# A block's MLP as half products beside the scores of the next block's attention, with four maxima a group there

## The chip, the cores and the metric

The program runs on one core of one Trainium2 chip. The metric is the device time of one execution in microseconds (us), as the median of several runs; lower is better. The engines named below are PE (TensorE, matrix products), DVE (VectorE), ACT (ScalarE), POOL (GpSimd) and SP (the queue that issues most transfers). PEld is the loading of weights into PE.

## The reference

The reference is one transformer layer with a norm ahead of each half. `x` has 2048 rows of 512 numbers. All matrices are float32.

```
h  = x + attention(layernorm(x), wqkv) @ wo     # 32 heads of 16, full softmax over 2048 keys
h2 = h + silu(layernorm(h) @ w1) @ w2           # w1: 512 x 1792, w2: 1792 x 512
```

The kernel keeps float32 accuracy by splitting each float32 matrix of the MLP into a high and a low float16 part, and it takes three products for one (high by high, low by high, high by low). The softmax subtracts a row's maximum, and the kernel finds that maximum by computing the scores once more with queries on the partitions.

## The kernel before

**Blocks, items and groups.** The 2048 rows of queries are four blocks of 512. An *item* is one block of queries with four heads: 8 items a block, 32 in all. An item has 16 *groups*, one for each 128 keys, so there are 512 groups, and the main loop at the end of the kernel function runs over them in order.

**What one group does.** `scores` computes four products of 128 keys by 512 queries, one for each head. Each contracts over 64 rows, and it lies on the lower half of PE's rows (partitions 0 to 63) or on the upper half (64 to 127) by its head. Two products on different halves can run at the same time. Each score is followed by an exponential on ACT that reads the product from PSUM and writes a float32 tile named `pt` of 128 by 512. `maximum` computes a product of another, later item on 48 rows of the other half (the names in the profile are ps<-ks,qs for it and ps<-qs,ks for the score), and DVE reduces it to maxima. `values` multiplies the four `pt` tiles of the group two back (LAG = 2) by the values, in four column strips of PE that run together, and adds the result up in one bank of PSUM for the 16 groups of an item. Up to three maxima stand in a group, by the rate that `maxima` works out from when each item's maxima are due.

**PSUM.** There are eight banks. Scores take turns in a ring of four (`st`), maxima in a ring of three (`sm`), and one bank holds the sum of `values`. A product waits until the reading of what stood in its bank is done.

**The pt tiles.** `pt_tile` hands out 16 slots (PTS), 8 in one pool and 8 in another, in the order in which the tiles are asked for.

**The output and the MLP of a block.** When a block's eight items are done, the first item of the next block has eight groups (c of 8 to 15) with output work between their scores: product with `wo`, residual, statistics, norm, transposition by DMA into `hts`. Then `mlp` runs alone, with no exponentials: 14 first products of 12 matmuls, a SiLU and a split for each, then 4 row tiles of 42 matmuls. Into this stretch pairs of maxima are woven, 386 in all for the three stretches. ACT changes its function table for SiLU and back. The stretch stands before groups 144, 272 and 400 (`marks`). The fourth block's MLP runs at the end of the program, in `finish_last`.

**Order.** Every engine's instructions are kept in the order in which the code records them, and the tile framework adds the semaphores. An engine runs its queue in order, so an instruction that waits holds those behind it. SP issues transfers in order as well.

Of the kernel before, what the change touches and what calls it, by code (L numbers as in the profile page):

```python
# [20 lines left out]
P = 128  # L21
S = 2048
D = 512
# [25 lines left out]
PTS = 16  # L49
# [16 lines left out]
JOINT = 2  # L66
AHEAD = 4
# [4 lines left out]
BESIDE = (138, 138, 110)  # L72
OUTPUT = 8

# [7 lines left out]

BURSTS_1 = ({f: 6 for f in range(FC) if f not in (6, 13)},) * 2 + ({f: 6 for f in range(FC) if f % 3 != 1},)
BURSTS_2 = 12, 12, 10
SPAN_2 = 12 * (FC - 2) - 3

MORE = 2, 2, 0
# [3 lines left out]
def attention_mlp_kernel(ctx: ExitStack, tc: tile.TileContext, x, wqkv, wo, w1, w2, out):  # L91
# [5 lines left out]
    def mm(*a, **k):  # L97
        tc.keep_in_program_order(nc.tensor.matmul(*a, **k))  # L98
# [12 lines left out]
    def act(fn, *a, **k):  # L111
        pin(getattr(nc.scalar, fn)(*a, **k))  # L112
# [80 lines left out]
    factors = const.tile([P, 14], F32, name="factors")  # L193
    sigma, inverse = factors[:, :4], factors[:, 4:8]
    w1_s, w2_s, wo_s, o_s = (sigma[:, n:n + 1] for n in range(4))
    h_f, g_s, out_f, wo_f, o_minus, o_twice = (factors[:, n:n + 1] for n in range(8, 14))
# [141 lines left out]
    def place_far(piece):  # L338

        i, _ = piece  # L340
        mt = small.tile([P, 32], F16, name="mt")
        dve("transpose", mt, split.pop(piece))
        issue = dma_beside if at["beside"] else dma
# [27 lines left out]
    at = {"item": 0, "done": 0, "half": 0, "step": 0, "due": 0, "attention": False, "group": None, "ready": 0, "next": 0, "blocks": True, "beside": False}  # L371
# [21 lines left out]
    def found_maxima(piece):  # L393
        g = at["group"]
        marked = g is not None and g + 1 in marks
        if g is None or marked or piece[1] is None and start_of(piece) - g > FAR:
            soon(WAIT + 1 if g is None or marked else CALM, place_far, piece)
            finish_max(piece, marked)
            return
# [62 lines left out]
    def scores(g, k, kind="st"):  # L462
# [7 lines left out]
        pts[g, k] = pt_tile("pt")  # L470
        act("activation", pts[g, k], ps, AF.Exp, scale=qk_f)


    with ExitStack() as pa:
# [57 lines left out]
        def set_factors():  # L532
# [4 lines left out]
            for to, a, f in ((h_f, inverse[:, :1], 1 / LN), (g_s, w1_s, 1 / 32.0), (o_minus, o_s, -1.0),  # L537
# [269 lines left out]
        def begin_scores(n):  # L807

            for _ in range(n):
                g, k = first_scores.pop(0)  # L810
                scores(g, k, "sm")
# [37 lines left out]
    gp = ctx.enter_context(tc.tile_pool(name="gp", bufs=2))  # L849

# [23 lines left out]
    def finish_item(i):  # L874
# [6 lines left out]
        elif i in FIRSTS:  # L881
# [98 lines left out]
    first_weights = {9: ("w1", 0), 12: ("w1", 1), 14: ("w1", 2), 15: ("w1", 3)}  # L980
    order = [(kind, f) for kind in ("w1", "w2") for f in range(FC)]

# [49 lines left out]
    def load_rows(b, t):  # L1032
        n = 4 * b + t
        hx[t] = cpool.tile([P, D], F32, name="hx", bufs=4)
# [41 lines left out]
    def add_seconds(b, t, ps, m=0, parts=1):  # L1076
# [4 lines left out]
        (dma_beside if m or at["beside"] else dma)(out[n * P:(n + 1) * P, cols], h[:, cols])  # L1081

    def pair_seconds(b, acc, tiles, f, gates):

        w2 = [ws.pop(("w2", k)) for k in (f, f + 1)]
        for t in tiles:
            rows = slice(t * P, (t + 1) * P)
            for k, ((gh, gl), (w2h, w2l)) in enumerate(zip(gates[f:f + 2], w2)):
                for x, w in ((gh, w2h), (gl, w2h), (gh, w2l)):
                    mm(acc[t], x[:, rows], w, start=f + k == 0 and w is w2h and x is gh, stop=f + k == FC - 1 and w is w2l)  # L1090
                    yield
            if f + 2 == FC:
                add_seconds(b, t, acc[t])

    def last_seconds(b, acc, gates, inserts={}, tiles=range(4)):

        w2 = [ws.pop(("w2", f)) for f in range(FC - len(gates), FC)]
        k = 0
        if b == NB - 1:
            h = rows_of(b, 3)  # L1100
            dve("scalar_tensor_tensor", h, acc[3], out_f, h, op0=ALU.mult, op1=ALU.add)
        for t in tiles:
            rows = slice(t * P, (t + 1) * P)
            parts = 1 + (4 * b + t == KC - 1)
            for m in range(parts):
# [3 lines left out]
                for (gh, gl), (w2h, w2l) in zip(gates, w2):  # L1109
                    for x, w in ((gh, w2h), (gl, w2h), (gh, w2l)):  # L1110
                        mm(ps, x[:, rows], w[:, cols], start=first and parts == 2, stop=w is w2[-1][1])
                        first = False
                        k += 1
                        if k in inserts:
                            inserts[k]()
                add_seconds(b, t, ps, m, parts)

    def mlp(b):

        ahead = [(g, m ^ (g % 2)) for g in marks[b:b + 1] + [marks[b] + 1] for m in range(4)]  # L1120
        weights = iter(order[5:] + order[FC:])

        def next_weights():
            for kind, f in weights:
                load_weights(kind, f)
                return

        def some_scores(n):
            for _ in range(n):
                scores(*ahead.pop(0), "sm")  # L1130

        gates = []
        lay_out(st=range(4), sm=attention_banks)
        for f in range(FC):
            tick()
            next_weights()
            w1h, w1l = (w.rearrange("p (c n) -> p c n", n=P) for w in ws.pop(("w1", f)))
            ps = space[:, f % 2, :]
            n = BURSTS_1[b].get(f, 0)
            if f == 0:  # L1140
                burst(n, 4, 6, 2)
                n = 0
            weave(product(ps, lambda c: w1h[:, c, :], lambda c: w1l[:, c, :],
                          lambda c: hth[:, c, :], lambda c: htl[:, c, :], DC),
                  {6: lambda: burst(n, 4, 6, 2)} if n else {})
            gates.append(gate(ps, "pool"))

        act("activation", small.tile([P, 1], F32, name="sw"), ident[:, :1], AF.Exp)
        acc = [space[:, n, :] for n in range(4)]
        positions = {SPAN_2 * (n + 1) // BURSTS_2[b]: n for n in range(BURSTS_2[b])}  # L1150

        def insert(k):
            half = 12 * FC // 2
            pairs = (4, 6)
            if not (half - 12 < k < half + 12 or k == SPAN_2):
                pairs = (2 if k < half else 0), 4, 6
            burst(2 * len(pairs), *pairs)

        k = 0
        for part in range(2):  # L1160
            for f in range(0, FC - 4 * part, 2):
                at["beside"] = part == 0 or f < 4
                tick()
                next_weights()
                next_weights()
                for _ in pair_seconds(b, acc, (2 * part, 2 * part + 1), f, gates):
                    k += 1
                    if k in positions:
                        insert(k)
        for _ in range(2):  # L1170
            tick()
            next_weights()
            next_weights()

        def scores_in(*ring):
            lay_out(sm=ring)
            some_scores(4)

        last_seconds(b, acc, gates[-4:], {6: lambda: scores_in(0, 1, 4, 5), 18: lambda: scores_in(6, 7, 4, 5)}, (2, 3))
        lay_out(sm=attention_banks[:3])  # L1180

    found = {}

    def output(b, n):

        if n < 4:
            ps = bank()
            weave(project_rows(n, ps), {6: lambda: singles(3)} if n < MORE[b] else {})
# [15 lines left out]
    def finish_block(b, pending):  # L1204

        act("activation", small.tile([P, 1], F32, name="sw"), ident[:, :1], AF.Silu)
        load_weights("w1", 4)
        for g in pending:
# [241 lines left out]
```

## Time and profile before

| what | us |
|---|---|
| median of 3 runs | 1593.77 (1593.76 to 1594.98) |
| span of the profiled execution | 1591.2 |
| PE busy | 1579.5 (99%) |
| DVE busy | 1386.9 (87%) |
| ACT busy | 1205.0 (76%) |
| POOL busy | 484.8 (30%) |

The page has one profiled execution. Its own time is its span from the first to the last instruction, 1591.2 us; the timed runs have 2.6 us more around that. In its rows a matmul counts as busy for as long as it is in the array, and matmuls overlap, so a busy PE isn't a PE at its peak. A row of the timeline has the start, the length, the engine, the line, the operation, what is written and read, and how many equal instructions it merges. The granted TensorE clock is 1.0 over the whole span.

### The profile page before, as it was taken

To read this page: it belongs to the slowest core of one execution; us is meant where nothing else is said; L and a number is where in the kernel's file an instruction comes from. 1 tells how busy PE (TensorE), PEld (TensorE's weight loads), DVE (VectorE), ACT (ScalarE), POOL (GpSimd) and SP (SyncE) were. 2 spreads that over 40 slices of the span, in tenths; PEclk is the share of its full clock that TensorE was granted. 3 is DMA by queue.
4 is the path that set the end of the run, shared out by engine and by line. 5 is a ranking of instruction groups with operands and counts; after the bars stand their busy time and mean duration, and the time that the engine had idled before them with its cause. 6 is when DMAs were issued, how large, how long until landed. Compare 5 with 4: busy or idle time off the path is not lost. (4 is left out here: it accounts for less than half of the span.)

```text
span 1591.2 us, 28420 instructions
## 1 busy us (share of the span) xinstructions
PE 1579.5 (99%) x10476; PEld 471.7 (30%) x10476; DVE 1386.9 (87%) x2045; ACT 1205.0 (76%) x2384; POOL 484.8 (30%) x764
## 2 busy tenths in 40 slices
PE   9999999999999999999999999999999999999999
PEld 6434222222223322222224322222224322222254
DVE  7999999999998889999988889999986889998432
ACT  6545799999964179999973179999974189999732
POOL 5643544544446101211146101211146101211200
PEclk9999999999999999999999999999999999999999
DMA  6667533443443511121243521112143511100232
GB/s 216 174 177 221 136 86 91 113 119 86 116 100 102 157 47 35 38 51 44 50 102 101 152 53 34 39 41 53 48 104 108 159 40 37 34 12 22 74 87 73
DMA packets 124099, 140.29 MB, mean 88 GB/s; under 512 B 41808, under 2 KB 78736, under 8 KB 123960
## 3 DMA queue, kind: packets, MB, share of 16 engines
q1 hardware_dynamic: 117744, 128.34, 30.5%
q10 hardware_dynamic: 6216, 10.15, 2.3%
q8 instruction: 82, 1.34, 0.4%
q14 instruction: 57, 0.47, 0.1%
HBM read 104.68 MB, written 24.85 MB: 81 GB/s over the span
## 5 line engine op out<-in xcount | busy, mean ns | idle before, releaser
L112 ACT ACTIVATE pt<-ps 128x512 f32<-128x512 f32 x2048 | 1009.3, 611 | 154.4 <-PE ps L98 154.0
L301 DVE TENSOR_REDUCE mx<-ps 128x1 f32<-128x512 f32 x1470 | 925.1, 684 | 48.2 <-PE ps L98 20.3
L98 PE MATMUL ps<-pt,va 128*17 128x512 f32 x4096 | 537.5, 598 | 1.1
L98 PE MATMUL ps<-qs,ks 64*128 64x512 f16 x2048 | 530.9, 379 | 1.5 <-DMA qs<-mn 0.4
L98 PE MATMUL ps<-ks,qs 48*128 48x512 f16 x2048 | 495.4, 380 | 2.6 <-ACT pvs L112 1.1
L299 DVE TENSOR_REDUCE mx<-ps 128x2 f32<-128x1024 f32 x289 | 334.9, 1219 | 43.8 <-PE ps L98 42.5
L98 PEld LDWEIGHTS <-ks 64*128 64x128 f16 x2048 | 149.3, 95 | 549.2 <-issue 432.5
L105 POOL TENSOR_TENSOR ri<-rc,minus 128x16 f32<-128x16 f32 x31 | 90.7, 2926 | 242.5 <-DMA rc<-dn 192.3
L98 PE MATMUL ps<-w,gh 128*128 128x512 f16 (+1 forms) x678 | 154.4, 378 | 0.0
L98 PE MATMUL ps<-hts,w 128*128 128x512 f16 (+1 forms) x708 | 153.3, 369 | 0.0
L98 PEld LDWEIGHTS <-qs 48*128 48x128 f16 x2048 | 126.1, 94 | 77.5 <-issue 61.3
L98 PEld LDWEIGHTS ps<-pt,va 128*17 128x17 f32 x4096 | 69.0, 95 | 225.7 <-issue 205.4
L112 ACT ACTIVATE g<-ps,factors 128x512 f32<-128x512 f32 x56 | 38.4, 686 | 125.0 <-PE ps L98 95.7
L105 POOL TENSOR_TENSOR mx<-mx 128x32 f32<-128x32 f32 x52 | 12.6, 241 | 386.4 <-DVE mx L301 379.8
L98 PEld LDWEIGHTS <-w 128*128 128x128 f16 x708 | 66.5, 98 | 78.6 <-issue 10.2
L98 PEld LDWEIGHTS <-gh 128*128 128x128 f16 x678 | 63.1, 98 | 82.9 <-issue 13.7
L112 ACT ACTIVATE ks<-ps 128x512 f32<-128x512 f32 x30 | 17.9, 598 | 50.5 <-PE ps L98 45.1
L115 DVE SCALAR_TENSOR_TENSOR gh<-g,factors,gh 128x512 f16<-128x512 f32 x14 | 10.5, 751 | 52.1 <-ACT gh L112 52.1
L105 POOL TENSOR_TENSOR sl<-ks,sh 128x512 f16<-128x512 f32 x30 | 34.7, 1157 | 51.5 <-ACT sh L112 38.1
L105 POOL TENSOR_TENSOR gh<-g,gh 128x512 f16<-128x512 f32 x42 | 48.6, 1156 | 3.5
L105 POOL TENSOR_TENSOR ot<-ot,den 128x512 f32<-128x512 f32 (+1 forms) x16 | 20.4, 1273 | 84.4 <-DMA den<-dr 75.8
L98 PE MATMUL ps<-xth,wqk_h 128*128 128x512 f16 x120 | 45.8, 381 | 0.0
(155 smaller groups left out, 919.7 us busy)
## 6 DMA issues: line engine op xcount, KB each, us to landing
w<-w2d SPq DMA_DIRECT2D x98, 256.0 KB
ks<-kd SPq DMA_DIRECT2D x120, 192.0 KB
w<-w1d SPq DMA_DIRECT2D x56, 256.0 KB
ks<-in_B_w_dram ACTq DMA_DIRECT2D x28, 256.0 KB
w<-in_B_w_dram SPq DMA_DIRECT2D x28, 256.0 KB
qs<-qd SPq DMA_DIRECT2D x128, 48.0 KB
kd<-sh SPq DMA_DIRECT2D x16, 256.0 KB
qd<-sh SPq DMA_DIRECT2D x16, 256.0 KB
```

The source lines that it names most:

```text
L98: tc.keep_in_program_order(nc.tensor.matmul(*a, **k))
L105: tc.keep_in_program_order(getattr(nc.gpsimd, op)(*a, **k))
L112: pin(getattr(nc.scalar, fn)(*a, **k))
L115: pin(getattr(nc.vector, fn)(*a, **k))
L299: pin(nc.vector.tensor_reduce(of, space[:, n:n + 2, :], axis=AX.X, op=ALU.max))
L301: pin(nc.vector.tensor_reduce(of[:, j:j + 1], space[:, n, :], axis=AX.X, op=ALU.max))
```

## The change

The three MLP stretches are gone. A block's MLP runs instead inside 112 groups of the next block, from the same three marks on (groups 144 to 255, 272 to 383, 400 to 511). They are called *MLP groups* here, and the other 176 *plain groups*.

Each product of the MLP over 128 rows is made of two *half products* over 64 rows each, which add into one bank (bank 3). In an even group six half products run on the lower row half, and in the odd group after it the same six run on the upper half. The scores of the two groups are sorted for this: the even group takes the four scores on the upper half, two of its own and two of the next group, and the odd group takes the four on the lower half. A group's matmuls are recorded as pairs, one from each half. With four maxima that makes seven such pairs, where before there were four.

Since two halves must not write a bank at one time, the first half product of a group waits for the exponential of the last score of the group ahead (`after`, the entry "fence"). Where a chain ends, ACT copies the bank out and the next chain's first half product waits for that copy.

The scores' ring has three banks in MLP groups. `PTS` is 12 rather than 16, in pools of 8 and 4 slots, since a tile `gates` for all of the SiLU's results takes room. SiLU is made from Tanh. Most of its work is on POOL, and so is the last addition of a row tile. The second weights are loaded once for each row tile, that is four times a block. An item's sums are copied out by ACT from item 9 on, by DVE before that.

`maxima` asks for up to four maxima a group everywhere, and for four in an MLP group wherever an item has them left.

PE, the first products of the first MLP before (`w` holds first weights, `hts` the normed rows, `qs0`/`ks0` are a maximum's queries and keys):

```order
L98 LDWEIGHTS qs0_100
L98 MATMUL ps_66<-ks0_99,qs0_100 128x512
L98 LDWEIGHTS w_5411 [waits DMAHW5_49,DMAHW7_49,DMAHW2_49,DMAHW0_49]
L98 MATMUL ps_66<-hts_1868,w_5411 128x512 [waits DMAHW1_49]
L98 LDWEIGHTS w_5411
L98 MATMUL ps_66<-hts_1868,w_5411 128x512
```

PE, one MLP group (155) after the change, from the values of group 152 on (`pt`, `va`); `qs1`/`ks1` are a maximum, `ks4`/`qs4` a score:

```order
L93 MATMUL ps_66<-pt_6108,va_109 17x512
...
L93 MATMUL ps_66<-pt_6159,va_109 17x512
L93 LDWEIGHTS qs1_102
L93 MATMUL ps_66<-ks1_101,qs1_102 128x512 [waits DVE_49]
L93 LDWEIGHTS ks4_107
L93 MATMUL ps_66<-qs4_108,ks4_107 128x512 [waits Activation_49]
L93 LDWEIGHTS w_5733 [waits Activation_49]
L93 MATMUL ps_66<-hts_1869,w_5733 128x512
L93 LDWEIGHTS qs1_102
L93 MATMUL ps_66<-ks1_101,qs1_102 128x512 [waits DVE_49]
L93 LDWEIGHTS w_5733
L93 MATMUL ps_66<-hts_1869,w_5733 128x512
```

Where a first product stood in one piece, its halves now stand between scores and maxima. The weight load with `[waits Activation_49]` is the fence: everything behind it on PE waits with it.

ACT in the same group (`g` is the copy of a finished chain; `pt_6214` is the first exponential of group 155, `pt_6237` the fourth, `pt_6247` the first of group 156):

```order
L107 ACTIVATE pt_6214<-ps_66 128x512 [waits PE_49]
L107 ACTIVATE pt_6221<-ps_66 128x512 [waits PE_49,Activation_49]
L107 ACTIVATE pt_6228<-ps_66 128x512 [waits PE_49,Activation_49]
L107 ACTIVATE g_6235<-ps_66,factors_84 128x512 [waits Pool_49]
L107 ACTIVATE pt_6237<-ps_66 128x512 [waits PE_49,Activation_49]
L107 ACTIVATE pt_6247<-ps_66 128x512 [waits PE_49]
```

The copy of a chain now stands between exponentials, where before it stood in a stretch without any.

The core of the diff:

```diff
-PTS = 16
+PTS = 12
+SHARE = 6
+    def after(ins, earlier):
+        tc.add_manual_dep(ins.ins, earlier.ins.name, mybir.DependencyInfo(
+            mybir.DependencyClass.Sync, mybir.DependencyReason.DATA), reason="row halves in one bank")
...
+    gates = gp.tile([P, FC, 2, 512], F16, name="gates", bufs=1)
...
+    def first_of(f):
+        w1h, w1l = (w.rearrange("p (c n) -> p c n", n=P) for w in take("w1", f))
+        for c in range(DC):
+            for w, x in ((w1h, hth), (w1l, hth), (w1h, htl)):
+                yield w[:, c, :], x[:, c, :]
+
+    def second_of(t):
+        rows = slice(t * P, (t + 1) * P)
         for f in range(FC):
...
+            w2h, w2l = take("w2", f)
+            for side, w in ((0, w2h), (1, w2h), (0, w2l)):
+                yield gates[:, f, side, rows], w
+
+    def end_first(f, ps):
+        z = gp.tile([P, 512], F32, name="g")
+        act("mul", z, ps, h_f)
+
+        def bend():
+            t = gp.tile([P, 512], F32, name="t", tag="oh")
+            act("activation", t, z, AF.Tanh, scale=0.5)
+            pool("tensor_scalar", t, t, 1.0, g_half, op0=ALU.add, op1=ALU.mult)
+            pool("tensor_tensor", t, t, z, ALU.mult)
+            pool("tensor_copy", gates[:, f, 0], t)
+            low(gates[:, f, 1], t, gates[:, f, 0], "pool")
+
+        soon(2, bend)
...
+    def half_product(j):
+        if j == 0:
+            current["open"].append(next(current["of"]))
+        lhs, rhs = current["open"][current["half"][j] - current["gone"]]
...
+        r = slice(64 * j, 64 * j + 64)
+        ins = mm(space[:, 3, :], lhs[r], rhs[r], start=current["half"] == [0, 0],
+                 stop=current["half"][1] == current["count"] - 1)
+        if "fence" in current:
+            after(ins, current.pop("fence"))
+        current["half"][j] += 1
+
+    def beside_products(g, n):
...
+        side = g % 2
+        heads = [(x, k) for x in (g - side, g - side + 1) for k in range(4) if head(x, k)[1] != side]
...
+        other = [("max", 1 - side)] * found[1 - side]
+        other = [step for m, of in enumerate(heads) for step in [("score", of), *other[m:m + 1]]]
+        count = current["count"] - current["half"][0] if side == 0 else current["half"][0] - current["half"][1]
+        same = [("max", side)] * found[side] + [("half", side)] * min(SHARE, count)
...
+        if current["half"][1] == current["count"]:
+            current["end"](space[:, 3, :])
+            current.clear()
+            waiting[3]()
+        else:
+            current["fence"] = waiting[3]()
...
+    beside = {g for m in marks for g in range(m, m + 4 * FC + 4 * FC)}
...
+        if g in beside:
+            at["due"] = 0
+            return max(0, min(most, ready - at["done"]))
...
         if g in marks:
-            finish_block(i // 8 - 1, (g - 2, g - 1))
+            begin_mlp(i // 8 - 1)
+            lay_out(st=range(3))
...
-        if g - LAG >= 0 and not (g in marks or g - 1 in marks):
+        if g - LAG >= 0:
             values(g - LAG)
```

More of the change, by code (lines that the diff above doesn't have):

```diff
@@ L342, in place_far @@
         dve("transpose", mt, split.pop(piece))
[L343 removed]
+        issue = dma
         for b in range(4):
@@ L370, in attention_mlp_kernel @@
     END = 64 * ITEMS
[L371 removed]
+    at = {"item": 0, "done": 0, "half": 0, "step": 0, "due": 0, "attention": False, "group": None, "ready": 0, "next": 0, "blocks": True}
     agenda, late = {}, {}
@@ L1202, in output @@
             found[n] = statistics(rows_of(b, n), LN)
[L1204 to L1208, printed above, removed]
-            values(g)
-        mlp(b)
     O = ot[(NB - 1) % 2]
```

240 lines of the change are left out of this document (115 added, 125 removed).

## The prediction

> **What bounds the kernel now.** I read the page's first part, then the chain of waits, then the timeline of one group.
>
> ```profile
> PE 1579.5 (99%) x10476; PEld 471.7 (30%) x10476; DVE 1386.9 (87%) x2045; ACT 1205.0 (76%) x2384; POOL 484.8 (30%) x764
> ```
> ```profile
> 1191.95 152.11 PE ps L98 x922
> ...
> 1345.99 60.91 PE ps L98 x464
> ...
> 1406.90 0.09 DVE mx L301
> ...
> 1428.00 58.94 ACT pt L112 x120
> 1486.94 0.04 issue
> ```
>
> The chain runs through PE's products for long pieces, and only near the end, where few maxima are left, through 120 exponentials (0.49 us each). So PE's queue sets the pace, and the chain never leaves it for DVE for longer than a reduction. Inside a group:
>
> ```profile
> 703.79 0.39 PE L98 MATMUL ps<-qs,ks 64*128 64x512 f16 x1
> 703.80 0.60 PE L98 MATMUL ps<-ks,qs 48*128 48x512 f16 x2
> ...
> 704.02 0.59 PE L98 MATMUL ps<-qs,ks 64*128 64x512 f16 x2
> ...
> 704.24 0.38 PE L98 MATMUL ps<-ks,qs 48*128 48x512 f16 x1
> ...
> 704.46 0.38 PE L98 MATMUL ps<-qs,ks 64*128 64x512 f16 x1
> ...
> 704.77 1.05 PE L98 MATMUL ps<-pt,va 128*17 128x512 f32 x8
> ...
> 705.75 0.39 PE L98 MATMUL ps<-qs,ks 64*128 64x512 f16 x1
> ```
> ```profile
> 704.25 1.89 DVE L301 TENSOR_REDUCE mx<-ps 128x1 f32<-128x512 f32 x3
> ```
> ```profile
> L112 ACT ACTIVATE pt<-ps 128x512 f32<-128x512 f32 x2048 | 1009.3, 611 | 154.4 <-PE ps L98 154.0
> L301 DVE TENSOR_REDUCE mx<-ps 128x1 f32<-128x512 f32 x1470 | 925.1, 684 | 48.2 <-PE ps L98 20.3
> ```
>
> A score and a maximum start together, and such a pair takes one *slot*: from 703.79 to 704.46 are three slots, 0.223 us each. From the last slot to the values are 0.31 us, from the values to the next group 0.98. So 3 x 0.223 + 0.31 + 0.98 = 1.96 us for a group. Three reductions of 0.684 us take 1.89, so each starts (1.89 - 0.684) / 2 = 0.60 after the last, and the first starts 0.45 after its product (703.80 to 704.25).
>
> **The stretches that go.** ScalarE's timeline shows each as a hole between exponentials:
>
> ```profile
> 470.49 2.14 ACT L112 ACTIVATE pt<-ps 128x512 f32<-128x512 f32 x4
> ...
> 565.22 2.06 ACT L112 ACTIVATE pt<-ps 128x512 f32<-128x512 f32 x4 [40.56 <-PE ps L98]
> ```
> ```profile
> 830.13 2.14 ACT L112 ACTIVATE pt<-ps 128x512 f32<-128x512 f32 x4
> ...
> 924.80 2.06 ACT L112 ACTIVATE pt<-ps 128x512 f32<-128x512 f32 x4 [40.49 <-PE ps L98]
> ```
> ```profile
> 1187.77 2.14 ACT L112 ACTIVATE pt<-ps 128x512 f32<-128x512 f32 x4
> ...
> 1277.13 2.06 ACT L112 ACTIVATE pt<-ps 128x512 f32<-128x512 f32 x4 [37.92 <-PE ps L98]
> ```
>
> 472.63 to 565.22 is 92.6 us, 832.27 to 924.80 is 92.5, 1189.91 to 1277.13 is 87.2: **-272.3 us**. The row of four (2.06 us, 0.611 the last) also gives (2.06 - 0.61) / 3 = 0.48 us from one exponential to the next.
>
> The 336 groups that take the MLP in took, before:
>
> ```profile
> 565.22:786.60 221.38, 221.12 (x1672) 50.01 (x1672) 208.31 (x337) 220.10 (x448) 36.75 (x68) 1.00 0.19 45
> 924.80:1146.26 221.46, 221.21 (x1672) 50.08 (x1672) 208.31 (x337) 220.18 (x449) 36.77 (x68) 1.00 0.19 45
> 1277.13:1497.50 220.37, 219.28 (x1623) 49.05 (x1622) 188.88 (x312) 218.30 (x444) 36.52 (x65) 1.00 0.16 39
> ```
>
> Together 663.2 us. The change wins if they, with what it adds elsewhere, stay under 663.2 + 272.3 = 935.5, which is 2.78 us a group.
>
> **An MLP group by its slots.** Four maxima, four scores and six half products make seven pairs: 6 x 0.223 + 0.31 + 0.98 = 2.63 us; in the last 19 groups, with no or one maximum left, six pairs and 2.41. A half product streams 512 columns as a score does, so I price it as one half of a slot. Four reductions at 0.60 are 2.4 us and four exponentials at 0.48 are 1.9, with two more ScalarE operations of about 0.7 for every four groups 2.3. By rate both fit in 2.63.
>
> **The fourth maximum waits.** Three banks serve the maxima, so the fourth product of a group needs the bank of the first. That reduction starts 0.45 after the group and ends at 0.45 + 0.684 = 1.13; with 0.05 to release PE (the chain's steps of issue are 0.04) the product can start at 1.18. In an MLP group its slot is the sixth, due at 5 x 0.223 = 1.12: 0.06 late, hence 2.69. In a plain group its slot is the fourth, due at 0.67: 0.51 late, and the values stand behind it. Counted in the built order, 50 plain groups outside the output have four maxima where before none had more than three. Between nothing (some other wait covers it) and 0.6 (the next group's third maximum is then late as well) I take 0.53: **+26.5**. Nine output groups have four too, where more work lies around it: 0 to 0.5 each, **+2**.
>
> **The tile that is not free.** This is the largest term. An odd MLP group asks for four `pt` slots of 12. Twelve are just enough, since values(g-3) freed four at the end of the group ahead. But the slots go round in order, 8 in one pool and 4 in the other, and the early scores of a next group break that order: the slots given to an even group s hold two tiles of s, freed at the end of s+2, and two of s+1, freed only at the end of s+3. Group s+3 is odd and gets these very slots whenever its turn falls on the pool of four, or on the second four of the pool of eight. That is so for g = 1 and 5 modulo 6: two groups of six, 112 in all. The semaphore values in the built program say the same: exponentials three and four of these 112 groups wait for the first and third product of the values at the *end of their own group*.
>
> What is late next: the values start at 2.69 - 0.98 = 1.71 and are done 1.05 later (the row at 704.77), at 2.76. The third exponential then starts at 2.79, the fourth 0.48 later and ends 0.61 after that, at 3.88. The next group's first half product waits for it (where a chain ends, for the copy behind the third, which is as long), and with it all of PE's queue. It starts at 3.92 rather than at 2.69 + 0.22 = 2.91, so 1.01 us late. In that group the fourth maximum is no longer late, which gives back 0.06: 0.95. Bounds: 0 if the wait were covered, 1.1 with the copy's 0.69 (the row of g, below) in place of 0.61. 112 x 0.95 = **+106**.
>
> In the other groups the fence costs nothing: the fourth exponential ends near 1.85 + 0.61 = 2.46 and the half product is due at 2.91. That cover is 0.45 us; if ScalarE were later by more, each 0.1 beyond would cost 22 us over the 224 other groups.
>
> So the 336 groups take 317 x 2.69 + 19 x 2.41 + 106 = 1004, against 663.2: **+341**.
>
> **The rest.**
>
> ```profile
> 450.76 2.06 ACT L112 ACTIVATE pt<-ps 128x512 f32<-128x512 f32 x4 [3.68 <-PE ps L98]
> ...
> 456.15 2.06 ACT L112 ACTIVATE pt<-ps 128x512 f32<-128x512 f32 x4 [2.82 <-PE ps L98]
> ...
> 460.88 2.06 ACT L112 ACTIVATE pt<-ps 128x512 f32<-128x512 f32 x4 [1.65 <-PE ps L98]
> ```
> ```profile
> 469.67 2.97 SPq L125 DMA_TRANSPOSE hts<-g  x2
> ...
> 475.18 4.06 PE L98 MATMUL ps<-hts,w 128*128 128x512 f16 x18
> ```
> ```profile
> L112 ACT ACTIVATE g<-ps,factors 128x512 f32<-128x512 f32 x56 | 38.4, 686 | 125.0 <-PE ps L98 95.7
> L105 POOL TENSOR_TENSOR gh<-g,gh 128x512 f16<-128x512 f32 x42 | 48.6, 1156 | 3.5
> ```
>
> Three maxima inside an output product made that group 5.39 us (450.76 to 456.15) against 4.73 for one without; four such products go: **-3**. The last two transpositions into `hts` are issued until 472.64, and before, the first product using them came at 475.18. Now it stands in the second slot of group 144, due near 472.6. Between 0 and 2.5 us late, three times: **+4**. POOL's part of a SiLU is at most four operations of 1.16 us for every four groups (10.8 us): hidden, and not needed until the second products, many groups later. The second weights come four times over, 256 KB a group of some 2.9 us or about 90 GB/s, on top of the 45 GB/s in the windows above. The page's slices reach more than that, so I count them as hidden:
>
> ```profile
> GB/s 216 174 177 221 136 86 91 113 119 86 116 100 102 157 47 35 38 51 44 50 102 101 152 53 34 39 41 53 48 104 108 159 40 37 34 12 22 74 87 73
> ```
>
>
> Sum: -272.3 + 341 + 26.5 + 2 - 3 + 4 = +98. The span goes from 1591.2 to 1689, and with the 2.6 us between span and median the time from 1593.8 to **1692 us**, slower by 6%.
>
> On the fence itself, the Trainium skill's page "TensorEngine Tiling (Array Packing)", in "Gotcha 1: PSUM Pressure", says that different row tiles can't access one PSUM bank at the same time and that software has to see to it; no run here shows that. Its "PSUM Bottleneck" says that tiling speeds TensorE up but not the reading of PSUM, so that this may become the bound. The rates above speak against that (2.4 and 2.3 against 2.63); where reading does bind here, it is by the number of banks.
>
> **Rivals.**
>
> *Every buffer is free in time* (faster). Then a group is as long as its slots: 317 x 2.63 + 19 x 2.41 = 880 us, +216 against 663.2. With -272.3 and -3 the span is 1532, the time 1535. For it: in the trace PE already runs with three maxima and DVE 0.60 apart and waits for neither. Against it: the two waits stand in the program, and nothing else delays the group by as much as they do. It decides where MLP groups average under (935.5 - 29.5) / 336 = 2.70 us; I have 2.99. If only the tile's wait were covered, it would be 1692 - 106 = 1586, faster by half a per cent.
>
> *Half products don't pair* with scores and maxima, say since accumulating into a bank excludes other writes. A group then has 13 slots, 12 x 0.223 + 0.31 + 0.98 = 3.97 us, and even without the tile's wait the groups take 336 x 3.97 = 1334: time near 1594 - 272 + 671 + 30 = 2020. Against it: pairs of two row halves are what the rows above show.
>
> *ScalarE falls further behind* (slower still): a tanh or a copy in front of the late exponentials adds up to 0.69 us to each of the 112 waits, 77 us: 1769. Against it: the tanh of a chain is recorded ahead of a group's first exponential, when ScalarE has nothing else.
>
> **How the numbers follow.** The forecast has 0.76, every buffer free or the tile's wait covered 0.12, no pairing 0.04, ScalarE further behind 0.08. The forecast's own range: 0.1 us on each of 317 groups is 32 us, and the tile's wait between 0.7 and 1.1 is -28 to +17; so 1640 to 1740. The range reaches a little to both neighbours, 1625 to 1750. A measurement of this kernel can tell about 0.2%. Slower: forecast, no pairing and ScalarE, less a little for sums of smaller errors: 0.87. Of the 0.12, most is faster: 0.10, and 0.03 within 0.2%.
>
> **What would show it.** Right: exponentials resume without a hole after groups 143, 271 and 399; MLP groups come in sixes, four near 2.7 us and two near 3.6; PE waits for ScalarE some 112 times for about 1 us; plain groups with four maxima take 2.5 us. Wrong: all MLP groups near 2.6 (waits covered) or near 4 (no pairing), or a PE that waits for transfers of `w`.

## The result, and the profile after

The changed kernel takes **1723.07 us** (median of 4 runs, 1722.68 to 1723.63) where the kernel before took 1594.10 beside it (4 runs, 1593.76 to 1594.98): a ratio of **1.081, 95% interval 1.080 to 1.083**. The prediction was 1692 in a range of 1625 to 1750. So the sign and the range held, and the size fell 31 us short.

The first part of the page of the changed kernel, and four of its groups of instructions:

```profile
PE 1585.2 (92%) x11486; PEld 475.5 (28%) x11486; DVE 1384.6 (80%) x2201; ACT 1247.1 (72%) x2403; POOL 576.1 (33%) x855
...
L303 DVE TENSOR_REDUCE mx<-ps 128x1 f32<-128x512 f32 x1842 | 1155.0, 684 | 194.8 <-PE ps L93 189.0
L107 ACT ACTIVATE pt<-ps 128x512 f32<-128x512 f32 x2048 | 1066.6, 605 | 324.1 <-PE ps L93 321.0
...
L93 PE MATMUL ps<-hts,w 64*128 64x512 f16 (+2 forms) x1212 | 285.6, 372 | 53.4 <-ACT g L107 26.0
L93 PE MATMUL ps<-w,gates 64*128 64x512 f16 x1008 | 247.4, 379 | 54.1 <-ACT pt L107 43.0
```

PE is busy as long as before (1585 us against 1579.5) in a span of 1720.9 us against 1591.2. The span grew by idle time of PE. Of its 136 us of idle time (1720.9 - 1585.2), 107 stand in front of the half products, most of it put down to ACT: the two last rows, 53.4 and 54.1 us. ACT and DVE for their part wait for PE. The waits of PE's queue (us in total, times, longest) give the same from the other side:

```profile
PE ps L93 <- ACT pt L107: 67.7, 75, 1.8
PE ps L93 <- ACT g L107: 34.2, 34, 1.3
PE ps L93 <- DVE mx L303: 15.0, 51, 1.3
PE ps L93 <- DMA hts<-g: 5.3, 3, 2.3
```

The holes of ScalarE are gone. At the first mark, where it had 92.6 us without an exponential, it has a few gaps, the longest of 2.5:

```profile
499.27 2.62 ACT L107 ACTIVATE pt<-ps 128x512 f32<-128x512 f32 x5
504.43 0.60 ACT L107 ACTIVATE pt<-ps 128x512 f32<-128x512 f32 x1 [2.53 <-PE ps L93]
```

What the MLP costs now stands in windows of the changed kernel: groups 2 to 127, all plain, and then the three runs of MLP groups, each from the first exponential of its first group. The columns are the window and its length, the busy time of PE, PEld, DVE, ACT and POOL with their instructions, the granted clock, the DMA share and GB/s.

```profile
179.26:453.83 274.57, 267.06 (x1926) 57.08 (x1926) 261.92 (x428) 254.39 (x506) 123.52 (x190) 1.00 0.36 99
501.26:843.33 342.07, 306.20 (x2465) 86.20 (x2467) 283.33 (x457) 254.24 (x487) 101.47 (x154) 1.00 0.30 81
892.88:1232.24 339.36, 303.63 (x2464) 85.78 (x2466) 281.38 (x453) 253.94 (x488) 101.48 (x154) 1.00 0.30 81
1282.76:1625.48 342.72, 302.59 (x2377) 84.39 (x2379) 237.76 (x393) 252.13 (x484) 91.97 (x113) 0.99 0.26 75
```

The plain stretch took, before:

```profile
179.38:427.31 247.93, 247.13 (x1881) 55.15 (x1882) 236.28 (x383) 247.52 (x505) 123.54 (x185) 1.00 0.41 108
```

The clock explains little of this. It was granted in full before. In the changed kernel it was granted at 0.50 in four stretches of 3.4 us, from 503.79, 1285.44, 1527.78 and 1585.81 on; the first of them:

```profile
503.79:507.20 3.41, 3.41 (x20) 0.82 (x16) 2.08 (x3) 1.79 (x3) 0.00 (x0) 0.50 0.24 88
```

At half the clock such a stretch loses at most half of its time, so the four cost at most 6.8 us of the difference. From the starts of the groups' first exponentials in both kernels the whole difference of the spans can be told part by part:

| part | before | after | difference | predicted |
|---|---|---|---|---|
| the three stretches | 272.3 | 0 | -272.3 | -272.3 |
| 336 MLP groups | 663.2 | 1024.1 | +361 | +341 and +4 |
| plain groups outside the output | 301.0 | 334.9 | +34 | +26.5 |
| six output groups, three times | 75.1 | 79.9 | +5 | +2 - 3 |
| the group ahead of each mark, and the end | | | +2.4 | 0 |
| span | 1591.2 | 1720.9 | +129.7 | +98 |

How a late MLP group looks: first PE, then ACT a few us on.

```profile
556.60 1.05 PE L93 MATMUL ps<-pt,va 128*17 128x512 f32 x8
557.58 0.39 PE L93 MATMUL ps<-ks,qs 48*128 48x512 f16 x1
...
558.81 0.39 PE L93 MATMUL ps<-hts,w 64*128 64x512 f16 x1 [0.83 <-ACT pt L107]
```
```profile
561.66 1.08 ACT L107 ACTIVATE pt<-ps 128x512 f32<-128x512 f32 x2 [0.46 <-PE ps L93]
564.03 0.60 ACT L107 ACTIVATE pt<-ps 128x512 f32<-128x512 f32 x1 [1.28 <-PE ps L93]
564.52 0.68 ACT L107 ACTIVATE g<-ps,factors 128x512 f32<-128x512 f32 x1
565.09 2.55 ACT L107 ACTIVATE pt<-ps 128x512 f32<-128x512 f32 x5
...
568.11 2.06 ACT L107 ACTIVATE pt<-ps 128x512 f32<-128x512 f32 x4
570.78 2.06 ACT L107 ACTIVATE pt<-ps 128x512 f32<-128x512 f32 x4 [0.61 <-PE ps L93]
```

The first half product should follow the maximum and score at 557.58 by one slot, at 557.80. It starts at 558.81. In ACT's rows a late group issues two exponentials (561.66), stands for 1.28 us until the values have read a tile, and issues the third at 564.03. Here a chain ends, so the copy `g` comes next and the fourth exponential is the first of the five at 565.09. The next group then begins 0.48 later, at 565.57: 3.91 us for the late group, 2.54 for the one behind it (to 568.11), 2.67 for the next one.

### The profile page after: what moved, and what is told of

It is laid out like the page before. It is cut to its first block, busy times and chain, and to the rows that moved or that the text cites. A ratio compares the mean times of both kernels' runs of the same rounds, so it can differ in the third digit from the quotient of the medians.

```text
span 1720.9 us, 31350 instructions
## 1 busy us (share of the span) xinstructions
PE 1585.2 (92%) x11486; PEld 475.5 (28%) x11486; DVE 1384.6 (80%) x2201; ACT 1247.1 (72%) x2403; POOL 576.1 (33%) x855
## 4 chain that ended last, share of the span: by engine, by line
PE 80%; ACT 7%; DVE 6%; issue 4%; DMA 2%; POOL 1%; SPq 0%; ACTq 0%; POOLq 0%; DVEq 0%
PE ps L93 79%; ACT pt L107 5%; DVE mx L303 4%; ACT g L107 2%; DVE mx L301 1%; PE ps L96 1%; DMA hts<-g 1%; DVE st L117 0%; POOL ri L100 0%; SPq L123 0%; DMA ks<-in_A_x_dram 0%; DVE gates L117 0%; DVE ks L117 0%; DVE pvs L117 0%; POOL wv_l L100 0%
## 5 line engine op out<-in xcount | busy, mean ns | idle before, releaser
L303 DVE TENSOR_REDUCE mx<-ps 128x1 f32<-128x512 f32 x1842 | 1155.0, 684 | 194.8 <-PE ps L93 189.0
L107 ACT ACTIVATE pt<-ps 128x512 f32<-128x512 f32 x2048 | 1066.6, 605 | 324.1 <-PE ps L93 321.0
L93 PE MATMUL ps<-qs,ks 64*128 64x512 f16 x2048 | 689.9, 381 | 5.3 <-ACT pt L107 2.6
L93 PE MATMUL ps<-ks,qs 48*128 48x512 f16 x2048 | 649.1, 380 | 16.1 <-DVE mx L303 15.0
L93 PE MATMUL ps<-hts,w 64*128 64x512 f16 (+2 forms) x1212 | 285.6, 372 | 53.4 <-ACT g L107 26.0
L93 PE MATMUL ps<-w,gates 64*128 64x512 f16 x1008 | 247.4, 379 | 54.1 <-ACT pt L107 43.0
L93 PEld LDWEIGHTS <-w 64*128 64x128 f16 (+1 forms) x1212 | 112.1, 95 | 154.1 <-ACT pt L107 33.8
L93 PEld LDWEIGHTS <-gates 64*128 64x128 f16 x1008 | 90.0, 94 | 172.0 <-ACT pt L107 65.5
L301 DVE TENSOR_REDUCE mx<-ps 128x2 f32<-128x1024 f32 x103 | 119.3, 1218 | 4.0 <-PE ps L93 3.5
L100 POOL TENSOR_TENSOR t<-t,g 128x512 f32<-128x512 f32 x42 | 53.6, 1275 | 3.5
```

Of the source, the lines that this page charges most:

```text
L93: return tc.keep_in_program_order(nc.tensor.matmul(*a, **k))
L100: tc.keep_in_program_order(getattr(nc.gpsimd, op)(*a, **k))
L107: ins = getattr(nc.scalar, fn)(*a, **k)
L301: pin(nc.vector.tensor_reduce(of, space[:, n:n + 2, :], axis=AX.X, op=ALU.max))
L303: pin(nc.vector.tensor_reduce(of[:, j:j + 1], space[:, n, :], axis=AX.X, op=ALU.max))
```

## Experiments

After the result my theory had three parts: the tile that is not free (112 groups) makes up most of the loss; the fourth maximum in plain groups most of what is left; the waits at the marks and in the output the rest. The rivals were that the half products themselves cost more than their slots, that ScalarE or VectorE has reached its rate, and that waits only move when one is removed.

**Tiles handed out as they come free.** The changed kernel, with one change: a slot comes up again in the order in which the tiles in it are freed, not in the order in which they were asked for.

```diff
-    taken = iter(range(10 ** 6))
+    unused, slot_of = list(range(PTS)), {}
-    def pt_tile(name, dtype=F32):
-        pool_of = pools[next(taken) % PTS >= EARLY]
-        return pool_of.tile([P, 512], dtype, tag="pt", name=name)
+    def pt_tile(name, dtype=F32, of=None):
+        n = unused.pop(0)
+        if of is None:
+            unused.append(n)
+        else:
+            slot_of[of] = n
+        return pools[n >= EARLY].tile([P, 512], dtype, tag=f"pt{n}", name=name, bufs=1)
...
+        unused.extend(slot_of.pop((g, k)) for k in range(4))
```

> The changed kernel, with its 12 tiles for exponentials handed out in the order in which the values free them, rather than in a fixed round of two pools; nothing else is touched and no wait is taken away by hand. Theory (tile not free): exponentials three and four of the 112 groups no longer wait for the values of their own group, the half product behind them starts about 1.0 us earlier each time, all MLP groups come near 2.7 us, and the time goes from 1723 to about 1612 us (112 x 1.0 less). Rival (the seven slots and the engines' rates are what the groups cost, and the lateness of the exponentials is only its sign): PE waits as long for something else, the time stays over 1700.

It took 1604.75 us (1601.37 to 1605.57) where 1612 was expected, a ratio to the kernel before of 1.0068 (1.0051 to 1.0085). The three windows of MLP groups:

```profile
501.32:806.16 304.84, 301.93 (x2465) 84.35 (x2467) 279.81 (x457) 252.19 (x487) 101.78 (x154) 0.99 0.34 91
855.18:1156.03 300.85, 299.60 (x2464) 84.09 (x2466) 277.96 (x453) 252.12 (x488) 101.73 (x154) 1.00 0.33 92
1205.77:1508.16 302.39, 296.42 (x2377) 82.74 (x2379) 236.00 (x393) 249.72 (x484) 92.21 (x113) 0.99 0.29 85
```

They sum to 908.1 us where the changed kernel has 1024.1, so the tile's wait cost 116 us, 1.04 for each of the 112 groups. The plain groups didn't move (274.57 us in groups 2 to 127, as without the edit). PE's waits for ACT fall from 101.9 us to 1.0. ACT's rows now come evenly:

```profile
696.03 2.06 ACT L107 ACTIVATE pt<-ps 128x512 f32<-128x512 f32 x4 [0.61 <-PE ps L93]
698.70 2.06 ACT L107 ACTIVATE pt<-ps 128x512 f32<-128x512 f32 x4 [0.61 <-PE ps L93]
```

2.67 us a group, with ACT waiting for PE: nothing but the slots sets the pace here. The same products, fences and exponentials run, so the half products as such aren't the loss.

**A strict round.** The opposite: the twelve slots one by one in the order of asking, in place of two pools.

```diff
-        pool_of = pools[next(taken) % PTS >= EARLY]
-        return pool_of.tile([P, 512], dtype, tag="pt", name=name)
+        n = next(taken) % PTS
+        return pools[n >= EARLY].tile([P, 512], dtype, tag=f"pt{n}", name=name, bufs=1)
```

> The changed kernel, with the twelve pt tiles as one strict round of single slots (before: a pool of eight and a pool of four, each handed on in its own order). By the order of the tiles alone, the third and fourth exponential of every odd MLP group, some 167 of them, then ask for a tile that the values product at the end of their own group frees, where it was 112. If each such wait costs what it cost in the changed kernel (1.00 us more for the group and the one behind it), it takes 55 more of them, +55 us: about 1778, and the MLP groups come in twos (about 3.6 and 2.7) rather than in sixes. Rival: the time of the MLP groups has another cause than these waits, and the kernel stays near 1723.

One run: 1781.03 us, against 1594.63 for the kernel before beside it. The MLP groups:

```profile
501.80:863.64 361.84, 308.29 (x2465) 86.78 (x2467) 284.78 (x457) 255.14 (x487) 101.68 (x154) 1.00 0.29 77
913.61:1271.93 358.32, 305.92 (x2464) 86.61 (x2466) 283.04 (x453) 255.22 (x488) 101.71 (x154) 1.00 0.28 77
1323.57:1683.85 360.28, 303.05 (x2377) 84.86 (x2379) 238.97 (x393) 253.05 (x483) 92.10 (x113) 0.99 0.25 72
```
```profile
PE ps L93 <- ACT pt L107: 101.7, 111, 1.8
PE ps L93 <- ACT g L107: 48.8, 49, 1.3
```

They sum to 1080.4, so 55 more waits cost 56.3 us, 1.02 each. PE waits for ACT 160 times, where it was 109. With none, 112 and 167 such groups the MLP groups take 908, 1024 and 1080 us. The number of waits sets the time, and the rival is out.

**No half products.** All half products but the last of each chain are left out. The fence goes with them; tiles, exponentials, maxima and copies stay.

```diff
-        ins = mm(space[:, 3, :], lhs[r], rhs[r], start=current["half"] == [0, 0],
-                 stop=current["half"][1] == current["count"] - 1)
-        if "fence" in current:
-            after(ins, current.pop("fence"))
+        current.pop("fence", None)
...
+        if current["half"][1] == current["count"]:
+            mm(space[:, 3, :], lhs[r], rhs[r], start=True, stop=True)
```

> The changed kernel with the half products left out but for the last one of each chain, so the output lacks the MLP of three blocks; the copies of the chains, tanh, POOL's work, the scores, the maxima (four a group) and the late tiles all stay, and the fence goes with the half products. The pairs stay seven (four scores and three maxima on one row half), so a group's slots are as before. Theory (the late tile costs through the fence): ordinary groups stay at 2.67, and the 112 late ones lose only what the scores wait for their banks, about 0.3 us each rather than 1.0; with 9 us of waiting for the first rows at the three marks also gone, 1723 - 78 - 9 = about 1636 us. Rival (the late tile costs by itself, whatever stands behind it on PE): about 1714. Rival (half products cost PE more than their share of the slots): ordinary groups fall below 2.5, time below 1600.

One run: 1681.4 us, neither number. The MLP groups and one of PE's waits:

```profile
501.38:823.73 322.35, 308.49 (x1811) 80.39 (x1812) 280.64 (x457) 251.05 (x487) 101.43 (x154) 1.00 0.32 86
873.27:1196.04 322.77, 308.00 (x1810) 80.38 (x1810) 278.91 (x453) 251.07 (x488) 101.44 (x154) 1.00 0.31 85
1246.55:1584.24 337.69, 319.68 (x1725) 77.98 (x1724) 236.78 (x393) 249.21 (x483) 92.00 (x113) 0.92 0.26 76
```
```profile
560.35 0.37 PE L93 MATMUL ps<-qs,ks 64*128 64x512 f16 x1 [0.47 <-ACT pt L107]
```

The fence is not the only way by which a late exponential reaches PE. Without it, late groups where no chain ends take 3.34 and 2.40 us, 0.4 more than two ordinary ones, as expected. But where a chain ends, the copy pushes the fourth exponential back, and the next group's third score finds its bank in the ring of three still being read (the row at 560.35). Those pairs take 3.91 and 2.40, 0.97 more, against 3.91 and 2.54 with the fence. My expectation had priced all of them like the first kind. Ordinary groups stay near 2.67 (565.25 to 567.93 in ACT's rows): the four scores and three maxima on one row half still make seven slots. So the rival that half products cost PE more than their share of the slots is out. In the third window the granted clock fell to 0.92 on average: it stood at 0.50 for 13.7 us from 1479.7 on and for 41.0 us from 1537.8 on. That is up to 27 us lost, enough for the 15 us that this window has over the other two. So this run says that the late exponential costs about as much with the fence as without where a chain ends, and that the fence adds about 0.6 where none does.

**One bank more for the maxima.** In plain groups the scores get three banks and the maxima four.

```diff
-    lay_out(st=range(4), sm=attention_banks[:3])
+    lay_out(st=range(3), sm=(*attention_banks[:3], 3))
...
-            lay_out(st=range(3))
+            lay_out(st=range(3), sm=attention_banks[:3])
...
-            lay_out(st=range(4))
+            lay_out(st=range(3), sm=(*attention_banks[:3], 3))
```

> The changed kernel with one PSUM bank moved, in plain groups alone, from the scores' ring (four to three) to the maxima's ring (three to four). MLP groups are untouched. Theory (a ring binds where the product after the last bank is due before the first bank is read): the fourth maximum no longer waits for the first reduction, but the fourth score now waits for the first exponential, which ends 1.03 us into the group, so it starts near 1.08 rather than 0.67 and every plain group without output takes about 2.37 us, with three maxima or with four. 157 x 2.37 = 372 against 157 x 2.19 = 344 now: about 28 us slower, 1750. Rival (VectorE's rate, not the ring, makes the groups with four maxima long): with one bank more the groups with four get shorter towards 2.1, the others stay at 1.96 to 2.0, and the time falls by 15 to 25 us to about 1703.

One run: 1753.84 us. Groups 2 to 127, and one of PE's rows there:

```profile
179.26:478.08 298.82, 267.38 (x1926) 60.23 (x1927) 262.24 (x428) 260.24 (x505) 123.78 (x190) 1.00 0.33 91
```
```profile
329.45 0.37 PE L93 MATMUL ps<-qs,ks 64*128 64x512 f16 x1 [0.25 <-ACT pt L107]
```

The fourth maximum doesn't wait any more (PE's waits for `mx` at L303 fall from 15.0 us to 3.0), and now every plain group waits for a score's bank: 298.82 / 126 = 2.37 us each, as expected. So the number of banks sets when a score can start. For the maxima this run doesn't tell the ring from VectorE's rate: three groups of 2.37 are 7.1 us, and ten reductions take 10 x 0.60 = 6.0, so both have time. There is no bank to spare, since eight are in use.

**The fourth product left out.** From here on the kernel with tiles handed out as they come free (1604.75 us) is the base. PE's fourth product for maxima is left out of plain groups that have four, output groups among them, and its reduction stays.

```diff
-            mm(space[:, n + m, :], qs[i % RING][64 * h:64 * h + 48, a, qt * P:qt * P + P],
+            at["stale"] or mm(space[:, n + m, :], qs[i % RING][64 * h:64 * h + 48, a, qt * P:qt * P + P],
...
+                    at["stale"] = n == 4 and m == 3
                     one_max(1 - head(g, k)[1])
+                    at["stale"] = False
```

> The kernel with tiles handed out as they come free (1604.75), without TensorE's fourth product for maxima in the plain groups; its reduction stays and reads what the bank held before, so some of the maxima belong to another step, and the output is not exact. If the fourth maximum costs because TensorE's queue stands at a bank that VectorE still reads, the 50 plain groups with four go from 2.2 (mean) to 1.96 or less and those behind them no longer wait: 0.6 to 0.7 each, some 35 us, about 1570. Rival: VectorE's four reductions (4 x 0.60) are themselves the rate, and the plain groups gain less than 10: about 1595 or more.

One run: 1590.84 us, 14 less than the base. The theory said 35 for the 50 plain groups with four, and the rival 10 or less. The plain groups outside the output took 5.7 us less, which is the rival's number; another 7.3 us came from the output groups. PE's rows, one reduction of VectorE, and the window of groups 2 to 127:

```profile
311.45 1.05 PE L93 MATMUL ps<-pt,va 128*17 128x512 f32 x8
...
313.47 0.37 PE L93 MATMUL ps<-ks,qs 48*128 48x512 f16 x1
313.77 1.05 PE L93 MATMUL ps<-pt,va 128*17 128x512 f32 x8
```
```profile
312.73 0.68 DVE L303 TENSOR_REDUCE mx<-ps 128x1 f32<-128x512 f32 x1
```
```profile
179.33:448.85 269.52, 268.99 (x1885) 58.06 (x1886) 259.67 (x428) 253.01 (x506) 123.46 (x190) 1.00 0.37 101
```

41 products are missing in that window (1885 against 1926), and it is only 5 us shorter. The group without its fourth product takes 1.96 us, but the group behind it takes 2.32 (311.45 to 313.77), since its third maximum starts at 313.47: the fourth reduction runs from 312.73 to 313.41 and holds the bank that this product needs. The wait has moved by one group. VectorE's rate would give 6.0 us for three groups with 4, 3 and 3 maxima. Here they take 6.29 early in the window and 6.46 later on, where with the product they take 6.57 and 6.46; so in the later part leaving it out gains nothing. VectorE is nearly at its rate: its timeline merges 30 reductions from 296.36 on into one row of 18.85 us, 0.63 each. So my first account was wrong about the product: what costs is the fourth *reduction*. How much of that is VectorE's time, and how much the bank that it holds longer, this run doesn't separate.

**An item's sums copied by ACT throughout.** Up to item 8 DVE makes this copy, and then the group's fourth maximum stands behind it as well.

```diff
-        elif i > FIRSTS[0]:
-            act("copy", pvs, pv)
...
-            dve("tensor_copy", pvs, pv)
+            act("copy", pvs, pv)
```

> The kernel with tiles in the order of freeing, and ScalarE copying an item's sums out for the first nine items too (VectorE did it in the changed kernel). Theory: in the third group of each of these items the values wait 0.4 to 0.6 us for VectorE's copy, which stands behind four reductions; ScalarE reaches it at once, so 9 x 0.6 to 1.0 = 5 to 9 us less than the kernel with free tiles alone: about 1605 us. That is still slower than before the change (1594), since the fourth maxima in plain groups (+35 to +39), the wait for the first rows at the marks (+10) and 336 groups at 2.67 rather than 1.97 (+235) outweigh the 272 us of the stretches. Rival (ScalarE, which has the exponentials, is late instead): no change against the kernel with free tiles.

1600.80 us (1599.26 to 1602.11), a ratio of 1.0044 (1.0028 to 1.0061): 4 us less than without the edit, where 5 to 9 were expected. The runs of the two kernels overlap a little, but groups 2 to 127 took 2.6 us less:

```profile
179.30:451.30 272.00, 266.04 (x1928) 57.47 (x1927) 258.33 (x422) 256.96 (x513) 123.47 (x190) 1.00 0.37 100
```

**The output one group earlier.** On top of the last one, `OUTPUT = 7` in place of 8, so that the last transpositions land before the first half product needs them.

> The kernel of the run before (free tiles, ScalarE copies all sums; 1600.8) with the output of a block one group earlier (c of 7 to 14 rather than 8 to 15). Theory: at the marks the first half product waits for the last transpositions into hts, which made groups 144 and 145, 272 and 273, 400 and 401 about 4.4, 2.9 and 2.6 us longer than two ordinary ones less their two values; an output that ends one group earlier (2.4 us) takes most of that away: about 6 us less, 1595. Rival (the output's own inputs are late then): the products with wo wait for POOL's split of the rows, and what is gained at the marks is lost in the output groups: 1601.

One run: 1599.17 us. The first two MLP groups take 5.5 us where they took 9.6, but the first output group now waits for POOL's part of the item that has just ended:

```profile
472.68 0.90 PE L93 MATMUL ps<-wo_h,oh 128*128 128x512 f16 x2 [1.22 <-POOL oh L100]
```

Of the 8 us that the MLP groups gave, 5 went to the output groups. A part of those 8 is the clock, which stood at 0.50 for 3.4 us behind two of the marks in the run ahead and behind none here. The rival that waits only move was nearly right.

**At most three maxima in four output groups.** On top of that, one line:

```diff
-        most = 3 if at["step"] in late else 4
+        most = 3 if at["step"] in late or i in FIRSTS and OUTPUT < c < OUTPUT + 5 and g < 600 else 4
```

> The kernel of the run ahead of this with at most three maxima in the four output groups that hold a product with wo and statistics, so that the maxima taken out go to plain groups around them. Theory: in those groups the fourth maximum waits behind VectorE's statistics, up to 1.3 us (output groups of 6.32, 5.81 and 5.66 us where before the change there were 4.74); without it they come back to 4.74, eight groups 0.45 to 1.6 us shorter or 7 us, of which the moved maxima give back 0.5 each, 2 to 3 us. Together about 1590, that is 0.2% faster than before the change or the same. Rival (the work is VectorE's and is only moved): no change against 1595.

1598.07 us (9 runs, 1596.18 to 1599.02), a ratio of 1.0025 (1.0015 to 1.0035). That is 1 us less than the run ahead, where 4 to 5 were expected, and with one run there even this is not clear of noise: the maxima that were kept out stand in other groups and cost there. This is the fastest of the kernels that leave nothing out, and it is still a quarter of a per cent slower than the kernel before. No version that beats it was found.

## Why the prediction was right, and where it was off

Every term that missed came out larger than forecast, so no miss made up for another.

**The stretches that go**: right, -272.3 us as worked out from the holes.

**An MLP group by its slots**: right. Seven pairs were priced at 2.63 and 0.06 for the fourth maximum, 2.69 in all; the ordinary groups of the changed kernel and of the one with free tiles take 2.67. Half products pair with scores and maxima at the price of a score. The rival *half products don't pair* (2020) is out with that.

**The tile that is not free**: right in mechanism, place and count, short by 9% in size. The step put the first half product of the next group 1.01 us late, and the rows show 557.80 against 558.81. It put 0.95 on each of 112 groups; the run without the wait shows 1.04, and the 55 more of the run with 167 show 1.02: 116 us, not 106. Against two ordinary groups (5.34), pairs without the end of a chain take 3.27 and 3.02 (0.95 more) or 3.34 and 3.02 (1.02), and pairs with one 3.91 and 2.54 (1.11). That last is the upper bound of 1.1, with the copy's 0.69 in place of 0.61; I had sized all 112 by the shorter case.

**The last groups** were priced at 2.41 with six pairs. The 17 without a maximum take 2.62 or more (one 2.58) even with free tiles:

```profile
1478.51 2.06 ACT L107 ACTIVATE pt<-ps 128x512 f32<-128x512 f32 x4 [0.55 <-PE ps L93]
```
```profile
1479.46 1.05 PE L93 MATMUL ps<-pt,va 128*17 128x512 f32 x8
1480.63 0.39 PE L93 MATMUL ps<-w,gates 64*128 64x512 f16 x1
```

The fourth exponential ends at 1478.51 + 2.06 = 1480.57, and the half product starts at 1480.63, not at 1479.46 + 0.98 = 1480.44. The sentence "in the other groups the fence costs nothing" failed here: its cover of 0.45 us was worked out with a maximum's slot ahead of the half product and a seventh pair, and these groups have neither. 0.2 us on each of 17 groups, and some groups of 3.02 (2.69 on average), make 5 us.

**The fourth maximum waits**: right in mechanism, but sized for its own group alone. That group costs 2.49 - 1.96 = 0.53, the very number. What was missed is who is late next:

```profile
303.62 1.05 PE L93 MATMUL ps<-pt,va 128*17 128x512 f32 x8
...
305.23 0.37 PE L93 MATMUL ps<-ks,qs 48*128 48x512 f16 x1
...
305.75 1.05 PE L93 MATMUL ps<-pt,va 128*17 128x512 f32 x8
...
307.93 0.37 PE L93 MATMUL ps<-ks,qs 48*128 48x512 f16 x1 [0.16 <-DVE mx L303]
308.24 1.05 PE L93 MATMUL ps<-pt,va 128*17 128x512 f32 x8
...
310.19 1.05 PE L93 MATMUL ps<-pt,va 128*17 128x512 f32 x8
```

From values to values: 2.13, 2.49 and 1.95 us, together 6.57 or 0.69 over three undisturbed groups. From about group 86 on they are 2.49, 2.01 and 1.96, or 0.58 over. The 0.17 in the group two behind was the "0.6" of my bounds, "the next group's third maximum is then late as well", from which I took nearly nothing. Where DVE also copies the sums the four's group takes 2.69 to 3.02. Together +34 and not +26.5. The rate should have warned me: I checked ten reductions against an MLP group's time only. In plain groups, three at 1.96 are 5.88 us, under the 6.0 that ten reductions take. The Trainium skill's page "TensorEngine Tiling (Array Packing)" says under "PSUM Bottleneck" that tiling doesn't speed up the reading of PSUM, which may then bind. I held this against the MLP groups, where the runs show nothing of it, and not against the plain ones, where the trace agrees (6.0 us of reading against 5.88 of products).

**Output groups**: they came out 5 us longer, where 2 more for the four maxima and 3 less had been forecast. One of the four's products waits 1.29 us behind VectorE's statistics:

```profile
490.00 0.37 PE L93 MATMUL ps<-ks,qs 48*128 48x512 f16 x1 [1.29 <-DVE mx L303]
```

**The wait at the marks**: bounded by 0 and 2.5 each, taken as 4 for the three. The first half product waits 2.33 us for the last transposition at the first mark, and 5.3 at the three together. I had taken the middle where the end was nearer. But the first two groups of the three runs of MLP groups take 9.4, 6.5 and 9.3 us where ordinary ones take 5.3: +9. Nearly all of the other 4 us is a term that the sum didn't have. Behind the waits at the first and third mark (2.33 and 2.06 us) the granted clock is 0.50 for 3.4 us, and a slot takes 0.43 us (504.15 to 504.58) rather than 0.22. Behind the second (0.91 us) it stays at 1.0. That the wait brings the lower clock is not shown.

```profile
503.55 0.38 PE L93 MATMUL ps<-hts,w 64*128 64x512 f16 x1 [2.33 <-DMA hts<-g]
```

**The rivals.** *Every buffer is free in time* is what the kernel with free tiles makes true of the tile alone. It was to be 1586; it is 1604.75, slower than before rather than faster, because of the terms above. *ScalarE falls further behind* did not happen: the copy behind the third exponential stands in the rows of the late groups, but adds about 0.1 us to a pair (1.11 against 0.95 to 1.02) and not 0.69, since the half product waits for the copy alone and then no longer for the exponential behind it.

The weights' transfers were counted as hidden, and PE waited for `w` once, 1.0 us.

## What to carry to other kernels

A ring of buffers that holds exactly as many as are needed still makes its user wait if it comes round in the order of asking while the buffers come free in another; work out, for the slot that comes next, the instruction that frees it. When a group of work gets one more item than its ring has buffers, price the item's release over the following groups too, and hold the reader's rate against the shortest group, not against the one that the change is about. And before work is folded into other work, count what it takes out and adds in the same unit: here half products take three more slots for 336 groups (225 us) for stretches of 272 us, which left little to pay for any wait.

## What the runs showed of the hardware that I had not expected

- A pair of matmuls of 64 rows (48 for a maximum) on different row halves takes 0.22 us whether its members are a score and a maximum, a half product and a score, or a half product and a maximum: seven such pairs and the values keep to 2.67 us over whole runs of groups.
- The column of PE's waits understates a ring that is short: it has 15.0 us for `mx` in the changed kernel, where the fours in plain groups cost 34. The row at 307.93 shows why: the product is 0.5 us late and has 0.16 of idle time, since most of the wait lies under the matmul ahead, which still counts as busy.
- The granted clock falls to 0.50 now and then: for 3.4 us at a time in the changed kernel, and in the kernel without half products for 13.7 and 41.0 us in the third run of MLP groups (0.92 on average), though fewer matmuls were issued there than in the changed kernel, which had 0.99. Why is open.
